# Chunk attention and a multiplicative FFN: tiles cut along the batches, more queries and keys loaded four tokens a partition, w1 and w2 awaited apart

## The chip, the cores and the metric

The kernel runs on one core of a Trainium2 chip. The metric is the device time of one execution in microseconds (us). The engines are TensorE (PE, matmuls, with PEld for its weight loads), VectorE (DVE), ScalarE (ACT), GpSimd (POOL, which here only issues loads) and SyncE (SP, which issues DMA transposes and stores). Sixteen DMA engines move the data.

## The reference, cut to what matters

```python
# q, k, v: (8, 8, 576, 64) float32: 8 batches, 8 heads, 576 tokens, 64 wide
q_c = q.reshape(B, H, 9, 64, D)                       # chunks of 64 tokens, 9 to a batch
scores = (1 / sqrt(D)) * matmul(q_c, k_c.transpose(0, 1, 2, 4, 3))
scores = scores - max(scores, axis=-1, keepdims=True)
attn = exp(scores); attn = attn / (sum(attn, -1) + 1e-9)
x = matmul(attn, v_c)            # each chunk attends to itself alone
x = x.transpose(0, 2, 1, 3).reshape(4608, 512)
h = ((x @ w1) * (x @ w2)) @ w3   # w1, w2: 512 x 1024, w3: 1024 x 1024
out = h @ w_out                  # w_out: 1024 x 512, out: 4608 x 512 float32
```

## The kernel before, in words

**Work.** A chunk is 64 tokens of one batch, and there are 72 of them. Two chunks make a *group* of 128 tokens (36 groups, g = 0 to 35), four groups make a *tile* of 512 tokens (9 tiles). In the kernel before, chunks are numbered straight through, so that a batch of nine chunks is four and a half groups, and a tile is eight chunks in a row wherever batches end: tile 0 is chunks 0 to 7 of batch 0, tile 1 is chunk 8 of batch 0 and chunks 0 to 6 of batch 1.

**A group.** Its queries and keys are brought in by POOL with a cast to bf16, turned so that the head dimension lies on the partitions, and copied: keys to `kT`, queries into `qd`, which holds two heads block-diagonally. Then PE makes the scores (`p_sc`, 8 matmuls), DVE takes the maximum and subtracts it, ACT the exponential, DVE the sum and the scaling to `an`; `an` is turned (`at`), PE multiplies by v (`p_av`, 8 matmuls with weights from `vd`, two heads block-diagonally), and ACT or DVE copies the result to `xt`, a ring of 16 groups.

**Two ways of loading q and k.** `load_qk` (L275) brings a group's q and k as one DMA each, one token a partition, so that DRAM is read in pieces of one head row (64 floats); a group that lies across two batches takes two halves each. `load_quad` (L289) brings eight chunks of four heads in four DMAs (two of k, two of q) with four tokens in a row on a partition (256 floats in a piece). A quad is turned by PE at L380: 16 matmuls on 64-column weights for k, and as many for q, serve two groups of the other cut (four chunks, four heads each). With `NQ = 1` tile 0 alone uses quads. Groups 4 to 11 are loaded by `load_qk` and turned by PE at L418 (8 matmuls a group); groups from 12 on are turned by DMA transposes (L422), and `an` from group 16 on too (L428).

**A tile.** `add_tile` (L577) makes for each of eight column blocks j the products a = x w1 and b = x w2 (L589: two *blocks* of four 128x512 matmuls), which ACT and DVE multiply into `abT`, and then four output products of eight matmuls (L620) with w3o = w3 w_out, copied by ACT or DVE and stored by SP (L630). w3o is made once at the start, from eight blocks w3 (L545 turns, L556 multiplies: 64 matmuls).

**What sets the order.** `Plan.run` lays the whole program out before it is built: each operation has engines, a cost and a key, and a list scheduler with modelled DMA queues picks the order in which each engine gets its instructions (and, where two engines can do an operation, which one does). On the chip every engine runs its list in order and waits by semaphores. POOL's loads follow the hand-written list `LOADS`, then a loop of q, k and v. Eight loads at most are on their way on POOL: a load waits for the landing of the eighth before it. `FLOWN` is the time at which the plan thinks that the DMA engines start. Until the first `p_av` matmul the plan puts filling matmuls on zeros (L683) into PE's longer gaps.

**What an operation waits for.** `w12_got[j]` holds one load for both w1 and w2: the last DMA of `load_w12`, which is w2's second half. A product waits for it and for `x_done` of the tile's four groups. A `p_av` waits for the v of its batch, which `load_v` brings in two DMAs of 64 partitions with all nine chunks. Stores wait until the q and k of group 35 were loaded. Tokens of groups 0 to 15 are kept for the store in the buffers of w3, w_out and `rawq` once these are free, later ones in 18 buffers `o_sb`.

Of the kernel before, what the change touches and what calls it, by code (L numbers as in the profile page):

```python
# [30 lines left out]
FLOWN, QUEUED, LAG = 3.5, 3.4, 1.2  # L31
# [143 lines left out]
def kernel(  # L175
# [32 lines left out]
    NG = N_TOK // (2 * C)  # L208
    scale = 1.0 / math.sqrt(D)
# [4 lines left out]
    BUFS = {"raw": 6, "rawq": 2, "kqT": 4, "kT": 3, "qd": 3, "vd": 3, "sd": 2, "e": 2, "an": 4, "at": 6, "w3t": 2, "abT": 2,  # L214
            "a_sb": 3, "o_sb": 18, "xt": XT, "ffn": 6, "p_sc": 1, "p_av": 1}
# [53 lines left out]

    def chunks(g):  # L270
        return [divmod(2 * g + cc, NCH) for cc in range(2)]
# [17 lines left out]
    def load_quad(n, y):  # L289
        box = quads[n, y] = {"ops": []}  # L290
        c0 = 8 * n
        cut = min(8, (c0 // NCH + 1) * NCH - c0)
        parts = [(c0, 0, cut)] + ([(c0, cut, 8)] if cut < 8 else [])
        for w, src in ((1, k), (0, q)):
            for t in range(2):
                for c, i0, i1 in parts:
                    def emit(eng, w=w, src=src, t=t, i0=i0, i1=i1):
                        if "t" not in box:
                            box["t"] = rawqs[len(turned_in) % len(rawqs)]
                            turned_in.append(box)  # L300
                        b, c = divmod(c0 + i0, NCH)
                        h = NM * t + 2 * y
                        nc.gpsimd.dma_start(box["t"][i0 * C // R:i1 * C // R, w, t],
                                            src[b, h:h + 2, c * C:(c + i1 - i0) * C, :].rearrange("h (p r) d -> p h (r d)", r=R))
                    box["ops"].append(load(0.084 * (i1 - i0), 0.5 + 0.02 * (i1 - i0), emit, takes=() if box["ops"] else ("rawq",)))

    def load_v(b, y0, y1):
        for t in range(2):
            def emit(eng, t=t):
                nc.gpsimd.dma_start(vds[b % len(vds)][halves[t], 2 * y0:2 * y1, :, t * D:(t + 1) * D].rearrange("p m c d -> p (m c) d"),  # L310
                                    v[b, NM * t + 2 * y0:NM * t + 2 * y1].rearrange("h (c p) d -> p (h c) d", p=C))
            o = load(1.07 * (y1 - y0), 0.5 + 0.335 * (y1 - y0), emit, takes=() if b in v_first else ("vd",),
                     after=(zero_v[b % len(vds)],))
            v_first.setdefault(b, o)
            for y in range(y0, y1):
                v_got.setdefault((b, y), []).append(o)

    def load_w12(j0, j1):
        for dst, w in ((w1_sb, moe_w1), (w2_sb, moe_w2)):
# [6 lines left out]
        for j in range(j0, j1):  # L326
            w12_got[j] = o
# [34 lines left out]
    def add_group(g, kt, ks, ka, kv):  # L362
# [3 lines left out]
        bc = [divmod(8 * n + 4 * hf + i, NCH) for i in range(4)] if quad else chunks(g)  # L366
# [34 lines left out]
        def quad_av(eng):  # L401
            t = box["av"] = ps("p_av", [P, 2, 4, C])
            for cc, (b, c) in enumerate(bc):
# [173 lines left out]
    def add_tile(g0, n, kab, ko_):  # L577
# [33 lines left out]
        for tk, x0, x1 in cols:  # L611
# [104 lines left out]
```

## Time and profile before

| | |
|---|---|
| runs | 249.84, 248.67, 249.61 us, median 249.61 |
| profiled execution | 249.81 us, its span 248.0 us (1.8 us lie around the span) |
| PE busy | 239.6 us of the span (97%), 1801 matmuls |
| DVE, ACT, POOL busy | 173.8, 146.3, 100.0 us |
| granted PE clock | 1.00 in every stretch |
| DMA | 38.58 MB, mean 156 GB/s |
| PE L589 (x w1, x w2) | 576 matmuls, 134.9 us busy |
| PE L620 (output) | 304 matmuls, 67.6 us busy |
| first L589 matmul, last L620 matmul's end | 36.9 us, 244.9 us |

Busy times of matmuls overlap, because they are pipelined: a 128x512 matmul is listed with 379 ns, while a row of them starts one every 0.216 us (the chain of waits has eight of them in 1.73 us). So where PE is at work, its work is counted here by the chain's pieces, and not by the busy column.

### The profile page before, as it was taken

Reading aid. Unit: us, or ns where it says so; the run is one execution under the profiler, and the core shown is the slowest. Engines: PE = TensorE matmul, PEld = TensorE weight load, DVE = VectorE, ACT = ScalarE, POOL = GpSimd, SP = SyncE. Lnnn points to the kernel's source line nnn. Section 1 sums busy time; section 2 is a strip of 40 time slices with the busy share of each in tenths; the row PEclk is TensorE's granted clock in tenths of the full one; section 3 lists DMA queues with packets and bytes.
Section 4 is the critical chain, followed back from the end, with each engine's and each line's share of the span. In section 5 each row is a group of like instructions: output and inputs, shape, how many; then the busy total and the mean of one; then the engine's idle time right before and its main releaser. Section 6 shows DMA issues by size and latency. Waiting matters only on the chain.

```text
span 248.0 us, 4765 instructions
## 1 busy us (share of the span) xinstructions
PE 239.6 (97%) x1801; PEld 123.6 (50%) x1801; DVE 173.8 (70%) x315; ACT 146.3 (59%) x250; POOL 100.0 (40%) x127
## 2 busy tenths in 40 slices
PE   7699999899999999999999999999999999999994
PEld 2455665456555554545545455454454544444443
DVE  6287879768988878987887778868888862332310
ACT  8566756656876775576566655565677544323222
POOL 8755889969773482274227435400000000000000
PEclk9999999999999999999999999999999999999999
DMA  7999999999999999999999999999469994121114
GB/s 196 194 203 173 177 182 180 166 155 148 132 135 144 158 154 157 137 156 138 156 136 161 130 156 156 146 148 161 86 140 307 342 344 144 45 84 42 45 42 169
DMA packets 154310, 38.58 MB, mean 156 GB/s; under 512 B 141232, under 2 KB 148272, under 8 KB 154288
## 3 DMA queue, kind: packets, MB, share of 16 engines
q0 software_dynamic: 112016, 18.88, 104.0%
q1 hardware_dynamic: 41984, 18.88, 40.6%
q10 hardware_dynamic: 288, 0.52, 0.8%
q8 instruction: 14, 0.23, 0.4%
q14 instruction: 8, 0.07, 0.1%
HBM read 38.80 MB, written 9.44 MB: 194 GB/s over the span
## 4 chain that ended last, share of the span: by engine, by line
PE 79%; DMA 10%; POOL 7%; issue 1%; DVE 1%; ACT 1%; POOLq 0%
PE ffn L589 45%; PE ffn L620 25%; DMA vd<-in_v_dram 7%; POOL w_sb L322 4%; PE p_av L490 3%; PE p_sc L447 3%; DMA rawq<-in_k_dram 2%; POOL raw L284 2%; POOL vd L310 1%; PE ffn L479 1%; PE p_av L683 1%; PE ffn L418 1%; ACT w3t L246 0%; PE ffn L380 0%; DVE qd L248 0%
## 5 line engine op out<-in xcount | busy, mean ns | idle before, releaser
L589 PE MATMUL ffn<-xt,w_sb 128*128 128x512 bf16 x576 | 134.9, 379 | 0.0
L589 PEld LDWEIGHTS <-w_sb 128*128 128x128 bf16 x576 | 53.7, 98 | 57.6
L598 DVE TENSOR_TENSOR abT<-a_sb,ffn 128x512 bf16<-128x512 f32 x72 | 48.8, 682 | 35.0 <-PE ffn L589 33.9
L620 PE MATMUL ffn<-w3o_sb,abT 128*128 128x512 bf16 (+2 forms) x304 | 67.6, 368 | 0.0
L246 ACT COPY a_sb<-ffn 128x512 f32<-128x512 f32 x72 | 42.0, 585 | 35.6 <-PE ffn L589 35.3
L284 POOL DMA_DIRECT2D raw<-in_q_dram x36 | 30.6, 854 | 43.5 <-DMA kqT<-raw 25.6
L620 PEld LDWEIGHTS <-abT 128*128 128x128 bf16 x304 | 28.3, 98 | 30.1
L284 POOL DMA_DIRECT2D raw<-in_k_dram x36 | 30.8, 860 | 9.0 <-DMA vd<-in_v_dram 6.8
L468 DVE TENSOR_REDUCE ss<-e 128x8 f32<-128x520 bf16 x36 | 24.8, 689 | 4.5 <-ACT e L464 4.4
L452 DVE TENSOR_REDUCE nm<-p_sc 128x8 f32<-128x512 f32 x36 | 24.3, 676 | 4.7 <-PE p_sc L447 4.0
L464 ACT ACTIVATE e<-sd 128x512 bf16<-128x512 f32 x36 | 22.8, 634 | 4.6 <-DVE sd L460 3.5
L474 DVE TENSOR_TENSOR an<-e,rs 128x512 bf16<-128x512 bf16 x36 | 24.7, 685 | 0.4
L246 ACT COPY o_sb<-ffn 128x512 f32<-128x512 f32 (+2 forms) x18 | 9.7, 539 | 22.3 <-PE ffn L620 22.2
L246 ACT COPY qd<-kqT 64x512 bf16<-64x512 bf16 x36 | 22.1, 614 | 0.2
L460 DVE TENSOR_TENSOR sd<-p_sc,nm 128x512 f32<-128x512 f32 x32 | 21.8, 682 | 0.4
L246 ACT CAST xt<-p_av 128x512 bf16<-128x512 f32 x27 | 15.9, 588 | 9.1 <-PE p_av L490 7.3
L310 POOL DMA_DIRECT2D vd<-in_v_dram x16 | 18.6, 1173 | 1.7 <-DVE ss L468 1.0
L556 PE MATMUL ffn<-wo_sb,w3t 128*128 128x512 bf16 x64 | 15.7, 380 | 0.2
L490 PEld LDWEIGHTS <-vd 128*128 128x128 bf16 x256 | 11.4, 98 | 6.3 <-issue 0.6
L447 PEld LDWEIGHTS <-qd 128*128 128x128 bf16 x256 | 11.2, 98 | 5.7 <-ACT qd L246 0.5
L490 PE MATMUL p_av<-at,vd 128*128 128x64 bf16 x256 | 12.8, 193 | 0.5 <-DMA vd<-in_v_dram 0.5
L248 DVE CAST xt<-p_av 128x512 bf16<-128x512 f32 x9 | 6.2, 689 | 5.9 <-PE p_av L490 5.9
(53 smaller groups left out, 164.4 us busy)
## 6 DMA issues: line engine op xcount, KB each, us to landing
out_dram<-o_sb SPq DMA_DIRECT2D x19, 256.0 KB, 2.4
vd<-in_v_dram POOLq DMA_DIRECT2D x16, 288.0 KB, 12.1
raw<-in_q_dram POOLq DMA_DIRECT2D x28, 128.0 KB, 9.0
raw<-in_k_dram POOLq DMA_DIRECT2D x28, 128.0 KB, 8.6
w_sb<-in_moe_w_dram POOLq DMA_DIRECT2D x8, 256.0 KB, 8.3
w_sb<-in_moe_w_dram POOLq DMA_DIRECT2D x16, 128.0 KB, 5.4
out_dram<-w_sb SPq DMA_DIRECT2D x8, 256.0 KB, 4.5
out_dram<-wo_sb SPq DMA_DIRECT2D x4, 256.0 KB, 2.8
```

Of the source, the lines that this page charges most:

```text
L246: nc.scalar.copy(o, i)
L284: nc.gpsimd.dma_start(box["t"][r, w], src[b, :, c * C:(c + n) * C, :].rearrange("h p d -> p h d"))
L310: nc.gpsimd.dma_start(vds[b % len(vds)][halves[t], 2 * y0:2 * y1, :, t * D:(t + 1) * D].rearrange("p m c d -> p (m c) d"), v[b, NM * t + 2 ...
L452: nc.vector.tensor_reduce(nm[:, :, 0], box["sc"], axis=AX.X, op=ALU.max)
L460: nc.vector.tensor_sub(sd[:], box["sc"], box["nm"].to_broadcast([P, 8, C]))
L464: nc.scalar.activation(e[:, :, :C], box["sd"][:], ACT.Exp, scale=scale)
L468: nc.vector.reduce_sum(ss[:], box["e"][:], axis=AX.X)
L474: nc.vector.tensor_mul(an[:], box["e"][:, :, :C], box["rs"].to_broadcast([P, 8, C]))
L490: nc.tensor.matmul(t[:, m, cc, :], vds[b % len(vds)][:, m, c, :], box["at"][:, 2 * cc + y, u * C:(u + 1) * C], start=True, stop=True)
L589: nc.tensor.matmul(t[:, :w], wt[:, ki, j * P:(j + 1) * P], x[:, ki, :], start=(ki == 0), stop=(ki == KO - 1))
L598: nc.vector.tensor_mul(box["abT"][:, j, :w], box["as", j][:, :w], box["b", j][:, :w])
L620: nc.tensor.matmul(t[:, :x1 - x0], box["abT"][:, ki, tk * P:(tk + 1) * P], w3o_sb[:, ki, x0:x1], start=(ki == 0), stop=(ki == FO - 1))
```

## The change

- `rows` and the new `chunks` cut tiles along the batches. Tiles 0 to 6 and tile 8 are the first eight chunks of one batch each (tile 8 is batch 7); tile 7 (`LEFT`) gathers the ninth chunk of all eight batches. Each group of tile 7 has chunks of two batches, so its q and k come in halves (16 DMAs, as the four groups across two batches took before), and its output rows are stored in two DMAs of 64 rows each.
- v is held by tile. The eight ordinary tiles load it as before, with all nine chunks of the batch; tile 7 loads its ninth chunks again, in eight small DMAs.
- `NQ = 3`: tiles 0, 1 and 2 (groups 0 to 11) use quads. `rawq` has four buffers in place of two, which also keep four more groups of output, and `o_sb` has 12 in place of 18.
- `w12_got` has an entry for w1 and one for w2, and each product waits for its own.
- `LOADS` has another order, and `FLOWN` is 2.7 in place of 3.5.

In the changed file the lines from 206 on stand some 2 to 12 lower: L380 becomes L391, L589 L600, L620 L631, L310 L325, L322 L333.

On PE the order that the plan makes has before the first product of tile 0: all of w3o as before, four L391 turns of sixteen matmuls more (quads 1,0 and 1,1, each k and q) in place of three L418 turns of eight, and the same four `p_av` of tile 0. The plan's fillers are 14 at the start, then 4 (7 before) between the first quad's k and q, then 2, 2 and 3 (2, 1 and 1 before). The first part of POOL's list, with DMAs in brackets, is: quad 0,0 (4); w3 three times; w_out (1); w3; quad 0,1 (4); w3; quad 1,0 (4); w3 twice; v of batch 0 (2); w3; w1 and w2 columns 0-1 (4); quad 1,1 (4); columns 2-3 (4); v of batch 1 (2); columns 6-7 (4); columns 4-5 (4); quad 2,0 (4); quad 2,1 (4); q and k of group 12 (2); v of batch 2 (2). Each set of w1 and w2 columns has w1's two DMAs first.

```diff
-LOADS = [('quad', 0, 0), ('w3', 5, 6), ('w3', 6, 7), ('ident',), ('wo', 4, 8), ('w3', 1, 2), ('quad', 0, 1), ('w3', 4,
-         5), ('w3', 0, 1), ('w3', 2, 3), ('v', 0, 0, 2), ('qk', 4), ('w3', 7, 8), ('w3', 3, 4), ('qk', 6), ('qk', 5),
-         ('w12', 0, 2), ('w12', 2, 4), ('w12', 6, 8), ('qk', 7), ('w12', 4, 6), ('v', 1, 0, 2), ('qk', 8), ('qk', 9),
-         ('qk', 10)]
+LOADS = [('quad', 0, 0), ('w3', 5, 6), ('w3', 7, 8), ('w3', 4, 5), ('ident',), ('wo', 4, 8), ('w3', 1, 2), ('quad', 0,
+         1), ('w3', 0, 1), ('quad', 1, 0), ('w3', 3, 4), ('w3', 6, 7), ('v', 0, 0, 2), ('w3', 2, 3), ('w12', 0, 2),
+         ('quad', 1, 1), ('w12', 2, 4), ('v', 1, 0, 2), ('w12', 6, 8), ('w12', 4, 6), ('quad', 2, 0), ('quad', 2, 1),
+         ('qk', 12)]
-NQ = 1
+NQ = 3
-FLOWN, QUEUED, LAG = 3.5, 3.4, 1.2
+FLOWN, QUEUED, LAG = 2.7, 3.4, 1.2
...
+    def rows(n):
+        return [(i, NCH - 1) for i in range(B)] if n == LEFT else [(n - (n > LEFT), c) for c in range(NCH - 1)]
+
     def chunks(g):
-        return [divmod(2 * g + cc, NCH) for cc in range(2)]
+        return rows(g // 4)[g % 4 * 2:g % 4 * 2 + 2]
...
         for w, src in ((1, k), (0, q)):
             for t in range(2):
-                for c, i0, i1 in parts:
...
+                def emit(eng, w=w, src=src, t=t):
+                    if "t" not in box:
+                        box["t"] = rawqs[len(turned_in) % len(rawqs)]
+                        turned_in.append(box)
+                    h = NM * t + 2 * y
+                    nc.gpsimd.dma_start(box["t"][:, w, t], src[n, h:h + 2, :R * P, :].rearrange("h (p r) d -> p h (r d)", r=R))
+                box["ops"].append(load(0.672, 0.66, emit, takes=() if box["ops"] else ("rawq",)))
...
+            if n == LEFT:
+                for m in range(2 * y0, 2 * y1):
+                    def emit(eng, t=t, m=m):
+                        nc.gpsimd.dma_start(vd[halves[t], m, :B, t * D:(t + 1) * D],
+                                            v[:, NM * t + m, (NCH - 1) * C:, :].rearrange("b p d -> p b d"))
+                    part(0.48, 0.62, (m // 2,), emit)
...
-        for j in range(j0, j1):
-            w12_got[j] = o
+            for j in range(j0, j1):
+                w12_got[name, j] = o
...
-            dep = [w12_got[j]] + [x_done[g0 + i] for i in range(n)] + ([first] if j else [])
-            a = plan.add("PE", 0.216 * n, kab(j), mm("a", w1_sb), after=dep, lag=0.2,
+            dep = [x_done[g0 + i] for i in range(n)] + ([first] if j else [])
+            a = plan.add("PE", 0.216 * n, kab(j), mm("a", w1_sb), after=dep + [w12_got["a", j]], lag=0.2,
...
             def o_out(eng, tk=tk, x0=x0, x1=x1):
-                r0 = (g0 + tk) * P
-                nc.sync.dma_start(out[r0:r0 + P, x0:x1], box["os", tk, x0][:, :x1 - x0])
+                os, bc = box["os", tk, x0][:, :x1 - x0], chunks(g0 + tk)
+                for i, (b, c) in enumerate(bc if bc[0][0] != bc[1][0] else bc[:1]):
+                    r0, n = b * S + c * C, P if bc[0][0] == bc[1][0] else C
+                    nc.sync.dma_start(out[r0:r0 + n, x0:x1], os[i * n:(i + 1) * n])
```

More of the change, by code (lines that the diff above doesn't have):

```diff
@@ L208 @@
     NG = N_TOK // (2 * C)
+    LEFT = 7
+    assert TT == (NCH - 1) * C == B * C
     scale = 1.0 / math.sqrt(D)
@@ L212 @@
     f32 = mybir.dt.float32
-    BUFS = {"raw": 6, "rawq": 2, "kqT": 4, "kT": 3, "qd": 3, "vd": 3, "sd": 2, "e": 2, "an": 4, "at": 6, "w3t": 2, "abT": 2,
-            "a_sb": 3, "o_sb": 18, "xt": XT, "ffn": 6, "p_sc": 1, "p_av": 1}
+    BUFS = {"raw": 6, "rawq": 4, "kqT": 4, "kT": 3, "qd": 3, "vd": 3, "sd": 2, "e": 2, "an": 4, "at": 6, "w3t": 2, "abT": 2,
+            "a_sb": 3, "o_sb": 12, "xt": XT, "ffn": 6, "p_sc": 1, "p_av": 1}
     consts = ctx.enter_context(tc.tile_pool(name="consts", bufs=1))
@@ L365, in add_group @@
         n, y, hf = g // 4, g % 4 // 2, g % 2
-        bc = [divmod(8 * n + 4 * hf + i, NCH) for i in range(4)] if quad else chunks(g)
+        cs = [4 * hf + i for i in range(4)] if quad else [g % 4 * 2, g % 4 * 2 + 1]
         qd = qds[g % len(qds)]
```

55 lines of the change are left out of this document (23 added, 32 removed).

## The prediction

> **What bounds the kernel now.** I read the page's busy shares and slices first, then PE's waits, the timelines of PE and POOL in the first 55 us, and the chain.
>
> ```profile
> PE 239.6 (97%) x1801; PEld 123.6 (50%) x1801; DVE 173.8 (70%) x315; ACT 146.3 (59%) x250; POOL 100.0 (40%) x127
> ...
> PEclk9999999999999999999999999999999999999999
> DMA  7999999999999999999999999999469994121114
> ```
>
> PE is the bound, at a full granted clock. The chain of waits names PE L589 and L620 without a break from 53 us on: the output product of tile 0 is at 55.5, the last L620 matmul ends at 244.9. Adding up PE's pieces at the chain's own durations (eight 128x512 matmuls 1.73, eight score or p_av matmuls 0.23, four turns of `an` 0.22, eight L418 turns 0.45, sixteen L380 turns 0.59, eight w3 turns 0.46) gives 190.0 us of work between 54.6 and the end, where 190.3 pass. No time can be won there except by taking PE work away, and the change takes none away. What can be won lies before 54.6:
>
> ```profile
> 7.28 0.41 PE L380 MATMUL ffn<-ident,rawq 128*64 128x128 bf16 x8 [1.58 <-DMA rawq<-in_k_dram]
> 7.92 0.41 PE L380 MATMUL ffn<-ident,rawq 128*64 128x128 bf16 x8 [0.22 <-DMA rawq<-in_k_dram]
> 8.26 1.68 PE L683 MATMUL p_av<-zeros 128*128 128x512 bf16 x7
> 9.88 0.64 PE L380 MATMUL ffn<-ident,rawq 128*64 128x128 bf16 x16
> ...
> 12.10 0.41 PE L398 MATMUL p_sc<-kT,qd 128*128 128x64 bf16 x8 [0.60 <-DVE qd L248]
> ...
> 44.69 0.62 PE L418 MATMUL ffn<-ident,raw 128*128 128x128 bf16 x8 [0.72 <-DMA raw<-in_k_dram]
> ...
> 52.63 0.28 PE L490 MATMUL p_av<-at,vd 128*128 128x64 bf16 x4 [0.51 <-DMA vd<-in_v_dram]
> ```
>
> The first quad's q landed at 9.30 (its last DMA is issued at 3.48 and takes 5.8), yet its turn began at 9.9, behind seven fillers of 0.22. By the same adding up, from the first turn at 7.28 to 54.63 PE had 40.1 us of work in 47.4: it lost 2.1 up to 9.95, 1.7 up to 17.1 (first copies, w_out), 1.6 up to the first product at 36.9, and 1.9 in tile 0's sixteen blocks, where the q and k of group 7 and the v of batch 1 came late. That v was late because POOL was late:
>
> ```profile
> 26.89 2.63 POOL raw L284 x3
> 29.52 1.86 POOL w_sb L322 x3
> ...
> 42.30 1.14 POOL vd L310
> 43.44 9.05 DMA vd<-in_v_dram
> ```
>
> From 26.9 to 43.4 the chain runs through POOL's issues, one after the other (0.88 for a q or k, 0.65 for w1 or w2), with the v at their end.
>
> **PE work, added.** Groups 4 to 11 lose eight L418 turns (8 x 0.45 = 3.6) and get four quads' turns of k and q (8 x 0.59 = 4.7): +1.1 us on the bound, hidden by nothing. Score, p_av, copy and softmax instructions stay in number and size (quad copies of `qd` took 0.42 on DVE at 10.56, plain ones 0.42 in the mean). The number of fillers stays 25. The Trainium skill (TensorE: Matmul & The Clock Gate, Weight-path perf modes) says that fast weight load is on "when the number of weights is 128", and these turns load 64; its slow rate, columns/1.2 ns, would make sixteen turns 0.85 us, by which the added turns would cost 3.2 in place of 1.1 and the forecast below would be 250.5. The trace disagrees on the size (0.59 for sixteen), though its loads of 64 columns do take longer than those of 128 (110 ns against 98), and 0.59 is used.
>
> **When the loads land.** The spacing of landings in the trace (issue plus time to landing, of single DMAs): quad 0.66, w3 block 1.25, half of w_out 2.54, v DMA 2.14, w1 or w2 0.67, q or k of a group 0.85. These sums give 51.4 for v of batch 1 in the kernel before, where 52.5 is measured, so they are good to about 1 us. In the new order: first quad 9.3 as now; w3 at 10.5, 11.8, 13.0; w_out 15.5; w3 16.8; quad 0,1 k and q 18.1, 19.5; w3 20.7; quad 1,0 22.1, 23.4; w3 24.7, 25.9; v of batch 0 30.2; w3 31.5; columns 0-1 w1 and w2 32.9, 34.2; quad 1,1 35.5, 36.9; columns 2-3 38.2, 39.6; v of batch 1 43.9; columns 6-7 45.2, 46.6; columns 4-5 47.9, 49.2; quad 2,0 50.6, 51.9; quad 2,1 53.2, 54.6; group 12 56.3; v of batch 2 60.6 (before: 60.2 and 64.3). POOL's chain is cut: between the v of batch 0 and that of batch 1 it issued 20 us of instructions, now 9.
>
> **PE's new order against these.** Four fillers in place of seven end at 9.25, so the q turn starts at 9.3: 0.6 won. The first scores follow at about 11.6 (12.1 before), after three serial copies of `qd`. The second half of the first w3o product waits for w_out as before; the first turn of `an` comes at 17.4. Then 19.2 us of work (48 product matmuls, 5 w3 turns, 6 quad turns, 5 of `an`, 4 scores, 4 p_av) and 0.9 of fillers and the wait around them bring the first product of tile 0 to 37.6; on the way each load is there 0.3 to 0.9 before its use, only quad 1,1's q is 0.1 late. The sixteen blocks with two scores, three turns of `an`, three p_av and the turns of quad 2,0 are 16.8 us: 54.3. On the way block 9 needs w1 of columns 6-7 at 45.3 (landed 45.2), block 11 its w2 at 47.5 (46.6), block 12 w1 of columns 4-5 at 48.4 (47.9), block 13 its w2 at 49.5 (49.2), quad 2,0 is turned at 51.2 (50.6). Awaiting w1 apart is what lets blocks 9 and 12 start; with w2 awaited too block 9 would start at 46.6, 1.3 us later, most of what this stretch wins.
>
> At 54.3 the new order has done one `an` turn, two p_av and quad 2,0 more than the old one had at 54.63, and has no four L418 left but quad 2,1: 190.3 - 0.22 - 0.46 - 1.8 + 1.18 = 189.0 are left. PE would end at 243.3, not 244.9: **-1.6 us**, the added 1.1 paid. This counts almost no loss from 17 to 54, where the kernel before lost 1.6 and 1.9. From below: none of it comes back. From above: all 3.5 comes back, and the result is +1.9. The nearest row is 27 to 42 of the same trace, with loads there in time, where PE lost about 0.3; I take 0.2.
>
> **Later.** Scores of groups 12 to 17 need DMA transposes; their q, k and v land about 4 us earlier, PE comes 1.6 earlier: covered. One place is tight: `an` of group 16 was ready 5.7 after its scores and took 8.4 to turn on SP's queue; the plan now puts its p_av 13.4 after the scores (19.8 before). That is a wait of 0 to 0.7; I take 0.2. PE is in order, so the wait stops everything behind it once.
>
> Tile 7: eight small v DMAs more (halves land 0.42 to 0.48 apart: 3.4 us of DMA, about 5.6 of POOL's issues against 2.3), four stores more on SP (0.6 each). At nothing: POOL ends at 160 us, the v of batch 7 had landed 20 us ahead of its p_av, and SP issued a store every 5.2 us from 205 on. Without that cover they would cost up to 3.4 and 2.2. The four `o_sb` groups of tile 8 need stores of tile 5, 60 us before. The tail (last matmul 244.9, span 248.0) has the same instructions.
>
> **Sum.** The profiled execution took 249.81: -1.6 + 0.2 + 0.2 = -1.2 gives 248.6. That execution is 0.2 above the median of the runs, so the forecast for the median is **248.4**.
>
> **Rivals.** *The waits only move.* The new order was made for loads that land just in time, and DVE stays at some 85% (by my count 18 us of its work from 37.6 to 58.9). If the loads are 1 to 2 us later, or DVE delays an `an` or a freed buffer, PE loses 1 to 2 of the 1.6 and the time is 249.0 to 250.2. For it: slacks under 1 us; columns 4-5 land 2 us later than before. Against: POOL's chain is gone.
>
> *Eight in flight bind, and the kernel is slower.* POOL's load waits for the landing of the eighth before it; the trace shows this at 12.02 and 14.57. From columns 0-1 to quad 2,1 stand 28 small DMAs. With a time to landing of 5.0 (w1 and w2 at 34 us) plus 0.3 to wake POOL, eight in flight give one per 0.66, just what I used. The first quad took 5.8: 0.76 apiece, 2.5 late at the end, and after the slack 1.7 to 1.9 of wait, 249.9. From a time to landing of 6.1 on (0.80 apiece, 3.7 late, 2.9 of wait) it is slower by over 0.5%; at 6.5, 252.2. For it: quads behind others took 8.7. Against: that was in a full queue, which loses nothing.
>
> **How the numbers follow.** This kernel's runs spread over 0.5%, which is about what can be told from no change. Forecast 0.55 (247.6 to 248.9; 0.44 of it under 248.36), waits only move 0.25 (all within 0.5%), eight in flight 0.20 (250.8 to 252). Faster 0.44, same 0.36, slower 0.20. The range from 247.6, with no loss and the fillers' wait too, to 250.9 leaves out most of the last case.
>
> **What would show it.** Right: the q turn at 9.3, first L600 near 37.6, v of batch 1 landed near 44, tile 0's output product near 56 with three tiles' turns ahead, last L631 matmul near 243.7, and L391 groups of 16 in 0.59. Wrong: waits of PE on rawq or w1/w2 loads over 1 us between 20 and 56 (the rivals), POOL idle behind landings with DMA engines not full (eight in flight), or PE waits on `at` after 100 us.

## The result: one per cent slower, and the profile after

| | before | after |
|---|---|---|
| median of six runs each | 249.5 us (248.67 to 249.84) | 251.92 us (251.26 to 252.61) |
| ratio, 95% interval | | 1.0104 [1.0075, 1.0133] |
| profiled execution | 249.81 us | 252.45 us |
| its span, and what lies around it | 248.0 + 1.8 | 250.2 + 2.25 |
| last output matmul ends | 244.9 | 246.88 |

The forecast was 248.4, the range 247.6 to 250.9. The kernel became 2.4 us slower where 1.2 were to be won, and the time lies outside the range, in the direction that had a chance of 0.20, though not by the mechanism that had been given for it: that the number falls into that rival's 250.8 to 252 is chance. The ratios here and below leave out runs that lie more than 1.5% above the fastest of the same kernel, which are three of e5's twelve (253.56, 253.68 and 255.09 us).

The busy shares and slices on the page of the changed kernel:

```profile
PE 241.7 (97%) x1865; PEld 123.3 (49%) x1865; DVE 176.3 (70%) x321; ACT 143.5 (57%) x244; POOL 102.8 (41%) x135
...
PEclk9999999999999999999999999999999999999999
DMA  7999999999999999999999999995757997122114
```

PE is the bound as before, at the full granted clock (1.00); its busy time is 2.1 us longer. Where the time went is read from the timeline of PE (start, duration, and in brackets the idle time before it). These are the changed kernel's lines; L391 turns a quad, L556 turns a w3 block, L567 multiplies w3o, L600 is the product with w1 or w2:

```profile
8.13 1.04 PE L695 MATMUL p_av<-zeros 128*128 128x512 bf16 x4
9.10 0.64 PE L391 MATMUL ffn<-ident,rawq 128*64 128x128 bf16 x16
...
11.92 0.41 PE L409 MATMUL p_sc<-kT,qd 128*128 128x64 bf16 x8 [0.87 <-ACT qd L248]
...
17.34 0.39 PE L490 MATMUL ffn<-ident,an 128*128 128x128 bf16 x4
18.60 0.62 PE L556 MATMUL ffn<-ident,w_sb 128*128 128x128 bf16 x8 [0.87 <-DMA w_sb<-in_moe_w_dram]
...
24.69 1.04 PE L567 MATMUL ffn<-wo_sb,w3t 128*128 128x512 bf16 x4
25.65 0.64 PE L391 MATMUL ffn<-ident,rawq 128*64 128x128 bf16 x16
26.22 1.04 PE L567 MATMUL ffn<-wo_sb,w3t 128*128 128x512 bf16 x4
27.10 0.40 PE L409 MATMUL p_sc<-kT,qd 128*128 128x64 bf16 x8
...
28.19 1.06 PE L556 MATMUL ffn<-ident,w_sb 128*128 128x128 bf16 x16
29.09 0.81 PE L695 MATMUL p_av<-zeros 128*128 128x512 bf16 x3
30.40 0.39 PE L409 MATMUL p_sc<-kT,qd 128*128 128x64 bf16 x8 [0.51 <-DVE sd L468]
...
38.88 0.64 PE L391 MATMUL ffn<-ident,rawq 128*64 128x128 bf16 x16
39.45 2.76 PE L600 MATMUL ffn<-xt,w_sb 128*128 128x512 bf16 x12
...
46.42 2.19 PE L600 MATMUL ffn<-xt,w_sb 128*128 128x512 bf16 x8
48.45 0.40 PE L416 MATMUL p_av<-at,vd 128*128 128x64 bf16 x8
...
51.73 2.19 PE L600 MATMUL ffn<-xt,w_sb 128*128 128x512 bf16 x8
```

The q turn is at 9.10 and the first turn of `an` at 17.34, as forecast (9.3 and 17.4). Then four things are to be seen. At 18.60 PE had waited 0.87 for a w3 block by the idle column; counted from the end of the turn of `an` at 17.56 (17.34 and 0.22) it is 1.04. The product of four at 24.69 takes until 25.65, 0.96, where a turn of a quad stands behind it; the same four at 26.22 take 0.88 where scores follow. Between 29.09 and 30.40 PE did nothing for the result: three fillers, then a wait, for the scores of group 4. And the eight matmuls at 46.42 took 2.03 until the next instruction, where eight in a row take 1.73. So the first product of tile 0 came at 39.4 (forecast 37.6; before 36.9), and the sixteenth ended at 57.0 (forecast 54.3).

The chain that ended last, in order of time, no longer goes through POOL's issues to the v of batch 1, as it did before; that v landed at 45.37 in place of 52.5. It names what took their place:

```profile
7.37 11.18 DMA w_sb<-in_moe_w_dram
...
25.72 0.59 PE ffn L391 x16
26.33 0.59 ACT qd L248
26.94 0.42 DVE qd L250
27.37 0.77 DVE qd L250 x2
28.17 0.69 DVE nm L463
28.86 0.61 DVE ss L479
29.70 0.57 DVE sd L468
30.40 0.39 PE p_sc L409 x8
...
46.59 0.45 PE ffn L600 x2
47.06 0.70 DVE xt L250
47.80 0.81 PE ffn L600 x3
```

First a w3 load; then, behind the turn of the q of quad 1,0, four copies to `qd`, one on ACT and three on DVE, and behind them on DVE the maximum, a sum and the subtraction of earlier groups, because there is one buffer for scores (`p_sc`) and the subtraction is what frees it. And twice in tile 0's products (the second time at 52.79) a copy of *tile 1's* x (groups 4 and 6), on which those products do not depend by their arithmetic.

### The profile page after: what moved, and what is told of

Read it like the earlier page. It is cut to its first block, busy times and chain, and to the rows that moved or that the text cites. A ratio compares the mean times of both kernels' runs of the same rounds, so it can differ in the third digit from the quotient of the medians.

```text
span 250.2 us, 4918 instructions
## 1 busy us (share of the span) xinstructions
PE 241.7 (97%) x1865; PEld 123.3 (49%) x1865; DVE 176.3 (70%) x321; ACT 143.5 (57%) x244; POOL 102.8 (41%) x135
## 4 chain that ended last, share of the span: by engine, by line
PE 88%; DMA 4%; POOL 2%; DVE 2%; ACT 1%; issue 1%; POOLq 0%
PE ffn L600 49%; PE ffn L631 25%; DMA w_sb<-in_moe_w_dram 4%; PE ffn L567 4%; PE p_sc L458 2%; PE p_av L501 2%; PE ffn L391 2%; PE ffn L490 1%; PE p_av L416 1%; POOL rawq L303 1%; PE p_sc L409 1%; DVE qd L250 1%; ACT qd L248 1%; POOL w_sb L342 1%; PE ffn L556 1%
## 5 line engine op out<-in xcount | busy, mean ns | idle before, releaser
L600 PE MATMUL ffn<-xt,w_sb 128*128 128x512 bf16 x576 | 135.6, 379 | 0.3
L600 PEld LDWEIGHTS <-w_sb 128*128 128x128 bf16 x576 | 53.3, 98 | 57.6 <-issue 0.7
L631 PE MATMUL ffn<-w3o_sb,abT 128*128 128x512 bf16 (+2 forms) x304 | 67.6, 368 | 0.0
L248 ACT COPY a_sb<-ffn 128x512 f32<-128x512 f32 x72 | 42.0, 584 | 38.7 <-PE ffn L600 38.5
L631 PEld LDWEIGHTS <-abT 128*128 128x128 bf16 x304 | 28.7, 98 | 31.8
L289 POOL DMA_DIRECT2D raw<-in_q_dram x28 | 23.7, 851 | 33.6 <-DMA kqT<-raw 30.5
L289 POOL DMA_DIRECT2D raw<-in_k_dram x28 | 23.9, 857 | 6.7 <-DMA vd<-in_v_dram 6.4
L248 ACT COPY o_sb<-ffn 128x512 f32<-128x512 f32 (+2 forms) x15 | 7.9, 528 | 21.6 <-PE ffn L631 21.6
L248 ACT COPY qd<-kqT 64x512 bf16<-64x512 bf16 x32 | 19.7, 616 | 0.3
L325 POOL DMA_DIRECT2D vd<-in_v_dram x16 | 18.7, 1182 | 2.6 <-PE ffn L600 1.7
L471 DVE TENSOR_TENSOR sd<-p_sc,nm 128x512 f32<-128x512 f32 x24 | 16.4, 685 | 0.3
L250 DVE CAST xt<-p_av 128x512 bf16<-128x512 f32 x16 | 11.0, 687 | 8.0 <-PE p_av L501 6.5
L567 PE MATMUL ffn<-wo_sb,w3t 128*128 128x512 bf16 x64 | 16.3, 380 | 0.0
L248 ACT CAST xt<-p_av 128x512 bf16<-128x512 f32 x20 | 11.7, 587 | 5.5 <-PE ffn L600 2.9
L303 POOL DMA_DIRECT2D rawq<-in_k_dram x12 | 8.6, 722 | 7.0 <-DMA vd<-in_v_dram 2.4
L501 PEld LDWEIGHTS <-vd 128*128 128x128 bf16 x192 | 8.7, 98 | 5.0 <-issue 0.2
L333 POOL DMA_DIRECT2D w_sb<-in_moe_w_dram x16 | 9.9, 643 | 2.4 <-DMA vd<-in_v_dram 2.3
```

What stands on the lines that cost most here:

```text
L248: nc.scalar.copy(o, i)
L289: nc.gpsimd.dma_start(box["t"][r, w], src[b, :, c * C:(c + n) * C, :].rearrange("h p d -> p h d"))
L325: nc.gpsimd.dma_start(vd[halves[t], 2 * y0:2 * y1, :, t * D:(t + 1) * D].rearrange("p m c d -> p (m c) d"), v[b, NM * t + 2 * y0:NM * t + ...
L471: nc.vector.tensor_sub(sd[:], box["sc"], box["nm"].to_broadcast([P, 8, C]))
L567: nc.tensor.matmul(box["wp"][:], box["t"][:, ki, :], wo_sb[:, ki, :], start=(ki == wo_cut[0][0]), stop=(ki == wo_cut[-1][1] - 1))
L600: nc.tensor.matmul(t[:, :w], wt[:, ki, j * P:(j + 1) * P], x[:, ki, :], start=(ki == 0), stop=(ki == KO - 1))
```

## The experiments

Four reasons stood against each other, for the front of the kernel (up to the end of tile 0's products) above all: *the loads land late* (by my sums v and w1/w2 should have landed 1.4 to 1.9 us earlier than they did); *DVE's chain* of copies and softmax ahead of group 4's scores; *false waits*, in which products of tile 0 wait for the copy of tile 1's x; and *the parts*, that one of the three parts of the change is itself a loss. Later came the price of a quad's turn. Each ratio is to runs of the kernel before that were timed beside it (medians 249.23 us for e1 to e4, 249.22 for e5 to e8, 248.84 for e9 to e12, 249.70 for e13 to e15), so that the ratios, and not the medians, are to be compared. Where an edit changes what an operation waits for or which loads there are (e4 to e7, e12), the plan also lays out the whole order anew.

**False waits: x in four buffers (e1).** `xt` is one buffer for four tiles, and a quad's copy writes a strided piece of it, which stretches over columns of another tile.

```diff
-    xt = wpool.tile([P, NM, XT * P], bf, tag="xt")
+    xts = [wpool.tile([P, NM, TT], bf, tag=f"xt{i}", name=f"xt{i}") for i in range(XT // 4)]
```

> The changed kernel with xt as four buffers of one tile each in place of one buffer of four tiles; nothing else moves, the order on every engine stays. Theory X (false waits): in the changed kernel two products of tile 0 stand still in the middle of a block, at 47 and 53 us, until DVE has copied x of groups 4 and 6, which they do not read; a quad's copy is a strided region, and the wait is made for the whole stretch of the buffer between its ends. By X the two stops of 0.46 us go and some small ones later: -0.9 us or a little more, about 250.9. Rival C (DVE and ACT set the pace): PE comes 0.9 earlier to waits for copies and softmax that stay where they are; under -0.3 us.

Measured: 251.45 us (250.65 to 251.77), 1.0085 [1.0054, 1.0115] of before. On PE's timeline the two stopped groups of products are whole again:

```profile
45.48 1.89 PE L600 MATMUL ffn<-xt,w_sb 128*128 128x512 bf16 x7
...
50.48 1.89 PE L600 MATMUL ffn<-xt,w_sb 128*128 128x512 bf16 x8
```

From the first product to the end of the sixteenth it is 17.0 us, not 17.6. So the false waits are real, and cost 0.6 us in the trace; in the time 0.5 (1.0104 to 1.0085), which the intervals do not tell apart from nothing. They are about a sixth of the 3.5 us that were missing, and not the 0.9 that was expected of them. That it is the strided copy which does it is borne out by the kernel before: there plain copies of the next tile's x go into the same one buffer beside a tile's products, and no group of products stops in the middle.

**The same split in the kernel before (e8).**

> The kernel before with xt in four buffers, no order changed. Theory X: its x copies of other groups stand in the same way behind products, but all of tile 0's quads were copied before its products, and from 55 us on PE lost 0.3 us in all; so -0.3 to 0: 249.2 to 249.5. If the split itself helped in general (rival: it is no cure of the change's loss but of both kernels), -0.9 as in the changed kernel.

Measured: 249.1 us, 0.9986 [0.9971, 1.0002]. There the split gives nothing that can be told from no change: what fits is that the stretch overlaps only where quads of tile 1 are copied while tile 0's products run.

**Lighter loads (e2, e3).** Half of the columns of w_out's second half are not loaded but set to zero at the start; e2 is the changed kernel with this, e3 has the split as well.

```diff
-        nc.gpsimd.dma_start(wo_sb[:, k0:k1, :], moe_w_out.rearrange(...)[:, k0:k1, :])
+        nc.gpsimd.dma_start(wo_sb[:, k0:k1, :D_MODEL // 2], moe_w_out.rearrange(...)[:, k0:k1, :D_MODEL // 2])
...
+        nc.vector.memset(wo_sb[:, STAGED:, D_MODEL // 2:], 0.0)
```

> The changed kernel, but the second half of w_out is loaded with 256 of its 512 columns (the others are set to zero once at the start), so that all loads behind it land about 1.2 us earlier; no order changes. Theory L (the loads are late): in the changed kernel w3 block 1 lands at 18.55 in place of the 16.8 that I had added up, and everything behind is 1.1 to 2.1 us late, while the order left 0.3 to 0.9 us. By L the first product comes at 38.3 in place of 39.4 and the time falls by 0.9 to 1.3 us, to about 250.8. Rival C (serial copies and softmax on DVE and ACT before the score of group 4 at 30.4 set the pace): at most -0.3 us.

> Both of the edits before together: xt in four buffers, and half of the columns of w_out's second half left unloaded. If X and L each take their own stretch of the front, the gains add: about -2.0 us, 249.9. If both only bring PE earlier to one common wait (C), the sum is no more than the larger of the two.

Measured: e2 252.67 us, 1.0141 [1.0109, 1.0173]; e3 252.16 us, 1.0107 [1.0068, 1.0146]. Neither gained what was expected (250.8 and 249.9), and neither is a clean test: a quarter of `wo_sb` is cleared at the start, and the first quad's q landed 0.35 us later than in the changed kernel in e2's profile and 1.5 later in e3's. The 0.35 is no more than executions differ without this edit (8.55 in e9, 9.30 in before). What can be read is inside the profiles. In e2 the loads behind w_out landed 0.8 to 2.7 us earlier than in the changed kernel's profile up to the v of batch 1 (44.44; a w3 block at 15.83 in place of 18.55), and still the first product came at 38.6, where e1, with its loads not lightened, had it at 38.5. Counted from the first scores (12.25 in e2, 13.42 in e3, 11.83 in e1) it is 26.3 us in e2 and e3, and 26.7 in e1. So lighter loads were worth about 0.4 in the front, not the 0.9 to 1.3 that the loads alone should have given.

**Cleaner: DVE's order (e9), less of w3 (e10), both (e11).** All three have x in four buffers. In e9 the list of DVE is changed behind the plan, so that the two copies for group 5 no longer stand ahead of group 3's maximum, and the three fillers ahead of group 4's scores are left out:

```diff
+        late = [o for o in order if tag(o) == ("qd", 5)]
+        for o in late:
+            order.remove(o)
+        at = [tag(o) for o in order].index(("sd", 3)) + 1
+        order[at:at] = late
...
-                    fills = int((o.start - last - 0.2) / 0.25)
+                    fills = int((o.start - last - 0.2) / 0.25) if last < 20 else 0
```

In e10 w3's fourth block is loaded for 128 of its 1024 columns, and its turn reads the second block instead:

```diff
+            n = P if k0 == 3 else D_FF
+            nc.gpsimd.dma_start(w3_sb[:, k0:k1, :n], moe_w3.rearrange("(ko p) n -> p ko n", p=P)[:, k0:k1, :n])
...
+                nc.tensor.transpose(t[:, ki, :], w3_sb[:, 1 if ko == 3 else ko, ki * P:(ki + 1) * P], ident[:])
```

> The changed kernel with x in four buffers (251.45 us, first product of tile 0 at 38.5, sixteenth block's end 55.2) and one change of order on DVE: the two copies of qd for group 5 come behind the subtraction of group 3 instead of ahead of its maximum, and the three filling matmuls ahead of group 4's scores are left out. Theory 'DVE holds the front' (the scores of group 4, at 29.46, waited 1.3 us, fillers and wait together, for p_sc, which DVE emptied late because the copies stood ahead): scores of group 4 near 28.6, the first product near 37.7, the time near 250.6. Rival 'loads hold the front' (the q of quad 1,1 landed at 37.59 and its turn began at 37.93): group 4's scores are earlier by the same 0.9, but the wait comes back at the q turn of quad 1,1, the first product stays within 0.2 of 38.5 and the time within 0.3 of 251.4.

> The changed kernel with x in four buffers, of w3's fourth block only the first 128 columns loaded (that block's turn reads the second block instead, so the output is not the reference's): 1.1 us of DMA less, from 26 us on, and nothing else moved on PE, ACT or DVE. Loads hold the front: everything from the v of batch 0 on lands 1.1 earlier, the first product comes at 37.5 to 37.7 and the time is about 250.5. DVE holds the front: the first product stays at 38.4 to 38.5 and the time within 0.3 of 251.4.

> Both edits together (part of w3 not loaded, so the output is not the reference's). If DVE and the loads each hold the front at about the same time, each edit alone gives nearly nothing and both give the first product at 37.5, the sixteenth block's end at 54.2 and 250.3 us; if one of them alone holds it, this is that edit's time to 0.3 us.

Measured, with the first scores of each profile, since the first quad does not land at the same time in every execution (where a trace lacks the record of the first product's first matmul, as in e1 and e10, its place is 0.22 ahead of the first one listed):

| | time, ratio | first scores | group 4's scores | first product | from first scores to it |
|---|---|---|---|---|---|
| e1 | 251.45, 1.0085 [1.0054, 1.0115] | 11.83 | 29.46 | 38.5 | 26.7 |
| e9 | 251.09, 1.0092 [1.0068, 1.0115] | 11.38 | 28.34 | 38.0 | 26.6 |
| e10 | 250.73, 1.0075 [1.0053, 1.0096] | 12.03 | 29.38 | 38.4 | 26.4 |
| e11 | 250.69, 1.0071 [1.0052, 1.0090] | 11.93 | 28.74 | 38.2 | 26.3 |
| changed kernel | 251.92, 1.0104 [1.0075, 1.0133] | 11.92 | 30.40 | 39.4 | 27.5 |

In e9 group 4's scores are 0.7 earlier, counted from the first scores, and hardly any of it is left at the first product. PE's timeline of e9 shows where it went:

```profile
28.34 0.41 PE L409 MATMUL p_sc<-kT,qd 128*128 128x64 bf16 x8 [0.42 <-DVE sd L468]
28.63 1.04 PE L569 MATMUL ffn<-wo_sb,w3t 128*128 128x512 bf16 x4
29.83 0.40 PE L490 MATMUL ffn<-ident,an 128*128 128x128 bf16 x4 [0.16 <-DVE an L485]
...
37.43 0.64 PE L391 MATMUL ffn<-ident,rawq 128*64 128x128 bf16 x16
38.00 2.76 PE L602 MATMUL ffn<-xt,w_sb 128*128 128x512 bf16 x11
```

The next turn of `an` is late in its place (1.20 from 28.63 to 29.83, where the four matmuls are 0.87), and the last quad turn stands right behind its load, which landed at 37.38. So neither theory holds alone: each edit shortens the front by 0.1 to 0.3 us, both by 0.4 where 1.0 was expected, and the times of the three cannot be told apart. With both, the front needs 26.3 us where the forecast had 26.0 (11.6 to 37.6); from the first turn of `an` to the first product it is 20.9, the forecast 20.2. DVE's chain and the loads are two gates set close behind each other; they are not where most of the 3.5 us went. The one large wait for a load, 0.87 at 18.60, is the changed kernel's profile alone: that w3 block landed at 18.55 there, and at 16.3 to 16.8 in e1, e9, e10 and e11.

**The price of a quad's turn (e13, e14).** 32 more turns, one ahead of each product with w1 in tiles 3 to 6, written into the PSUM buffer that the product then overwrites; in e13 each is sixteen matmuls with 64 columns of weights, as at L391, in e14 eight with 128 columns, as at L418 of before.

```diff
...
+                    if name == "a" and 12 <= g0 < 28:
+                        tr = t.bitcast(bf)
+                        for i in range(8):
+                            for u in range(2):      # e13
+                                nc.tensor.transpose(tr[halves[u], i * P:(i + 1) * P], ident[:, u * C:(u + 1) * C], ident[:])
+                            nc.tensor.transpose(tr[:, i * P:(i + 1) * P], ident[:], ident[:])      # e14, in place of the two lines above
```

> The changed kernel with x in four buffers (251.4 us) and 32 more turns, one ahead of each product with w1 in tiles 3 to 6, where PE is the bound: sixteen matmuls with 64 columns of weights each, as a quad's turn has, written into the PSUM buffer that the product then overwrites. If a quad's turn costs 0.57 to 0.59, as the prediction took it, the time rises by 18.2 to 18.9 us to about 270; if it costs 0.67, because whatever stands ahead of it takes 0.10 longer, it rises by 21.4 to 272.8.

> The same with 32 turns of eight matmuls with 128 columns of weights each, as a turn of load_qk's groups has: 0.45 a turn by the rows, so 14.4 us more, about 265.8, by either theory. The difference to the run with 64 columns, divided by 32, is what one quad's turn costs above one plain turn: 0.12 to 0.14 by the prediction's rows, 0.22 with the gap.

Measured: e13 272.09 us, 1.0914 [1.0869, 1.0959]; e14 265.35 us, 1.0615 [1.0567, 1.0663]. From the first product to PE's last matmul it is 206.6 us in e1, 228.3 in e13, 220.9 in e14: 0.68 for a turn with 64 columns, 0.44 for one with 128, a difference of 0.23 (by the ratios 0.65, 0.41 and 0.23). The rows on PE's timeline, e13 and then e14:

```profile
112.10 0.64 PE L603 MATMUL ffn<-ident 128*64 128x128 bf16 x16
112.67 1.90 PE L605 MATMUL ffn<-xt,w_sb 128*128 128x512 bf16 x8
...
114.64 1.89 PE L636 MATMUL ffn<-w3o_sb,abT 128*128 128x512 bf16 x8
116.46 0.64 PE L603 MATMUL ffn<-ident 128*64 128x128 bf16 x16
```

```profile
114.03 1.89 PE L635 MATMUL ffn<-w3o_sb,abT 128*128 128x512 bf16 x8
115.76 0.61 PE L602 MATMUL ffn<-ident 128*128 128x128 bf16 x8
116.20 1.89 PE L604 MATMUL ffn<-xt,w_sb 128*128 128x512 bf16 x8
```

Eight output matmuls are listed with 1.89 in both, but the turn with 64 columns begins 1.82 after they began, the turn with 128 columns 1.73 after. So the turn lengthens what stands ahead of it by 0.09 to 0.10, which no idle column shows; with the 0.57 from its own start to the next start that is 0.67. (Behind nine of the 32 turns e13's timeline lists an idle 0.16; there the record of the next product's first matmul is missing, seven listed for eight or three for four, so this is no wait.) The prediction's 0.59 is the turn's own piece in the chain and leaves the lengthening out. The two runs differ in the number of instructions as well as in the width of the weights, so they give the price of a turn and not which of the two sets it.

**Group 16's p_av later (e15).** To take away the reason for the one wait that the prediction called tight, e9's program with the p_av of group 16 and its copy behind three more blocks.

```diff
+        av, x = ([tag(o) for o in order].index((n, 16)) for n in ("av", "x"))
+        later = [i for i in range(av + 1, len(order)) if order[i].engine == "PE"][3]
+        pair = [order[av], order[x]]
+        order[later + 1:later + 1] = pair
+        order = [o for i, o in enumerate(order) if o not in pair or i > later]
```

> The changed kernel with x in four buffers and the copies of group 5 later (251.1 us), and the p_av of group 16 with its copy moved behind three more blocks on PE (2.6 us). In the profile of the run without this move PE waited 0.77 us at 107.4 for the DMA transpose of group 16; in other profiles of this order 0 to 0.17. If that wait is in most runs, the time falls by 0.4 to 0.8, to about 250.5, and the scatter shrinks; if it is rare, the time stays at 251.1.

Measured: 251.39 us, 1.0076 [1.0046, 1.0105], against 1.0092 [1.0068, 1.0115] for e9: not told apart. The wait for the transpose is gone from the profile, and another stands 4 us behind. From PE's timelines, e9:

```profile
107.44 0.39 PE L501 MATMUL p_av<-at,vd 128*128 128x64 bf16 x8 [0.77 <-DMA at<-an]
```

and e15:

```profile
112.98 0.39 PE L458 MATMUL p_sc<-kqT,qd 128*128 128x64 bf16 x8 [0.95 <-ACT e L475]
```

The loss came back at the scores of a later group: the same work, from the output product at 101.95 in e9 or 100.80 in e15 to the second one after it (at 114.17 and 113.21), takes 12.2 us in e9 and 12.4 in e15, and 11.3 in the changed kernel's profile (103.13 to 114.42), where neither wait is there. So by execution this place costs 0 to about 1 us.

**The parts.** e4 is the changed kernel with w1 and w2 awaited together:

```diff
-            a = plan.add(..., after=dep + [w12_got["a", j]], ...)
+            a = plan.add(..., after=dep + [w12_got["b", j]], ...)
```

> The changed kernel with one wait for both w1 and w2 again: each product of x w1 waits for w2's last load too; the loads keep their order, PE's order in tile 0 changes a little with the plan. The prediction's working said that awaiting w1 apart saves 1.3 us at block 9. In the profile w2 of columns 6-7 landed at 48.1 and block 9 stood at 47.8 for a false wait, so theory X says that the part was worth 0.3 to 0.8 us: 252.2 to 252.7. By the prediction's step: 253.2.

Measured: 253.19 us, 1.0147 [1.0118, 1.0176]. Awaiting them apart is worth 1.1 us by the ratios (1.3 by the medians) inside the change, as the prediction's step had it (1.3); the two intervals overlap a little.

e7 is the kernel before with nothing but this part:

> Only the third part: the kernel before with w1 and w2 awaited apart. In its profile the products of tile 0 lost 1.9 us, 0.9 of it to a load of q and k and 0.7 to the v of batch 1, neither of which moves; w1 and w2 landed before use. So 249.5, within 0.3 us. Rival: the plan moves products forward and takes up the gaps: -0.5 us.

Measured: 250.76 us, 1.0066 [1.0042, 1.0090]. Alone the same part is a loss of 1.6 us, where nothing or a small gain was expected. The plan now draws four of tile 0's products ahead of w3o's last four (the first comes at 35.9, 0.9 earlier than in before), and PE then waits for scores, which in before waited for nothing (the waits of PE in e7):

```profile
PE p_sc L447 <- DVE sd L460: 1.0, 1, 1.0
```

In e7's profile PE's last matmul ends 0.8 later than before's. The same wait, 1.01 at 39.91, stands in the profile of e12, below, which has this part with before's loads too.

e5 has the new cut of the tiles alone (the changed code with quads for tile 0 only, before's load order, buffers and `FLOWN`, w1 and w2 awaited together), e12 the same with w1 and w2 awaited apart, e6 the kernel before with `NQ = 3`, four `rawq`, twelve `o_sb`, and the new load order and `FLOWN`, but the old cut.

```diff
-NQ = 3
+NQ = 1
-FLOWN, QUEUED, LAG = 2.7, 3.4, 1.2
+FLOWN, QUEUED, LAG = 3.5, 3.4, 1.2
```

> Only the new cut of the tiles: the changed kernel with quads for tile 0 alone, the loads in the order of the kernel before, w1 and w2 awaited together, o_sb and rawq as before. Tile 7's eight small v loads and its stores in halves are in it. The prediction put the cut at nothing: 249.5, within 0.3 us. Rival: the 1 MB of extra v and the halves cost DMA time that PE waits for: 250 to 251.

> Quads for tile 0 alone and the loads in the order of before, but tiles cut along the batches and w1 and w2 awaited apart. The cut alone (with both awaited together) gave 251.3 with a wide scatter; awaiting apart gained 1.3 inside the changed kernel and cost 1.3 alone in the kernel before. If the cut costs 1.8 and awaiting apart is bad with the old loads: 252.6. If awaiting apart gains with the new cut: 250.0. What the changed kernel's 251.9 stands above or below it is what the quads of tiles 1 and 2 with the new load order are worth; by the prediction they gain 1 us or more, by the rows of the turns (0.67 each with the gap ahead of it) they cost 1.8 of PE work against 3.6 taken away by nothing.

> Only the quads: the kernel before with its old cut, but quads for tiles 0 to 2, the new order of loads, FLOWN 2.7, four rawq and twelve o_sb. w1 and w2 are awaited together. Quads that lie across two batches are loaded in more and smaller DMAs. Theory: the quads with their loads carry the whole loss (1.1 us of PE turns and 1 to 2 us of late loads): 251.5 to 253, as the changed kernel or worse. If the cut carries it: 249.5 to 250.

| | new cut | quads for three tiles, new loads | w1, w2 apart | time, ratio |
|---|---|---|---|---|
| e5 | yes | | | 251.33, 1.0074 [1.0049, 1.0099] |
| e7 | | | yes | 250.76, 1.0066 [1.0042, 1.0090] |
| e6 | | yes | | 256.83, 1.0304 [1.0278, 1.0330] |
| e12 | yes | | yes | 253.59, 1.0190 [1.0153, 1.0226] |
| e4 | yes | yes | | 253.19, 1.0147 [1.0118, 1.0176] |
| changed kernel | yes | yes | yes | 251.92, 1.0104 [1.0075, 1.0133] |

Every part alone is slower than before, and so is every pair that was run; e5, e6 and e7 all came out slower than expected. The cut costs 1.8 us by itself, where the prediction had it at nothing. e5's twelve runs (all of them in the median, nine in the ratio) scatter from 249.75, the level of before, to 255.09, and the profiled one is the last of these: it waited 2.7 us for an `an` and 1.6 for a group's k, and whether the others did is not known. So where the cut's cost arises stays open. In e12 PE waits for the transposes of group 16:

```profile
109.33 0.39 PE L501 MATMUL p_av<-at,vd 128*128 128x64 bf16 x8 [1.18 <-DMA at<-an]
```

and its tiles 3 to 8 take 113.6 us from first product to first product, where before's and the changed kernel's both take 112.2. On the new cut, with w1 and w2 apart, the quads and loads gain 2.1 us (1.0190 to 1.0104); with w1 and w2 together they cost 1.8 (1.0074 to 1.0147), and on the old cut 7.6. So what a part is worth depends on the others, but the three together are no better than the cut or the wait apart by itself (1.0104 beside 1.0074 and 1.0066, the intervals overlap), and 2.4 us behind the program that they replace.

## Why the prediction was wrong, step by step

The prediction's sum for the profiled execution was 248.6 (PE's end at 243.7, with the two allowances of 0.2), and it took 252.45. The 3.8 us between, by the prediction's own steps:

| step | forecast | profile after | missed |
|---|---|---|---|
| first product of tile 0 | 37.6 | 39.45 | 1.85 |
| from it to the sixteenth's end | 16.7 | 17.6 | 0.9 |
| from there to PE's end, allowances included | 189.4 | 189.8 | 0.4 |
| from PE's end to the span's | 3.1 | 3.3 | 0.2 |
| around the span | 1.8 | 2.25 | 0.4 |

**The step that failed** is "This counts almost no loss from 17 to 54 ... I take 0.2". The sum was made of PE's pieces laid end to end, with the loads as the only thing that could come between, and the 0.2 was taken from a stretch of 15 us of the old program that had no quad turns and no copies of a second quad in it. The bound "From above: all 3.5 comes back, and the result is +1.9" was none: the profiled execution took 2.6 more than before's, because what came was for the most part not the old losses. From the first turn of `an` to the first product PE took 22.1 where 20.2 were forecast, and the 1.9 us are 1.0 for the w3 block at 18.60, 0.4 at group 4's scores (1.3 for 0.9) and 0.5 for six quad turns (0.67 for 0.59). The 0.9 in the sixteen blocks are 0.6 of false waits, 0.2 of two turns' lengthening and 0.1 without a name; the 0.4 behind them, 0.2 of two more turns and a third stop, 0.19 at 83.05 behind a copy of x, that e1's trace does not have. That is one execution, 0.5 above the median, and its 1.0 for the w3 block is not in four other profiles of the same order. The items one by one:

- **The term of the turns was mis-sized.** "Four quads' turns of k and q (8 x 0.59 = 4.7)" against "8 x 0.45": +1.1 was counted. A turn costs 0.68 in place (e13) and a plain one 0.44 (e14): +1.9. For the six turns ahead of the first product, the two in the sixteen blocks and the two of quad 2,1 that is 0.9 us that the sums left out. The lengthening was in the trace of before, too (there L556 multiplies w3o, L380 turns a quad and L418 a plain group): four matmuls on w_out at 18.77 ran until the quad's turn at 19.74, 0.97, and the four at 32.27 until the plain turn at 33.14, 0.87. I had looked at the turn and not at its neighbour.

```profile
18.77 1.04 PE L556 MATMUL ffn<-wo_sb,w3t 128*128 128x512 bf16 x4
19.74 0.64 PE L380 MATMUL ffn<-ident,rawq 128*64 128x128 bf16 x16
...
32.27 1.04 PE L556 MATMUL ffn<-wo_sb,w3t 128*128 128x512 bf16 x4
33.14 0.61 PE L418 MATMUL ffn<-ident,raw 128*128 128x128 bf16 x8
```

  The Trainium skill (TensorE: Matmul & The Clock Gate, Weight-path perf modes) ties the fast weight load to 128 weights. The prediction weighed this rule and set its 250.5 aside on the size of one row; the rule had the direction right, and the estimate that the prediction worked out from the Trainium skill's columns/1.2 ns (same page, LDWEIGHTS: 0.85 for sixteen loads) is above the 0.68 that the runs show. No run here shows that the fast load is the reason, since the turns differ in the number of instructions too.
- **False waits**, 0.6 us in the trace (46.42 and 51.73), shown by e1. The prediction did not have them in any case: tile 1's x is now copied by quads while tile 0 is being multiplied from the same buffer.
- **Group 4's scores** came 1.3 us after the last useful instruction, where "0.9 of fillers and the wait around them" were counted, and the loads stood close behind; e9 to e11 show that the two together are worth 0.4 in the front.
- **The landing sums** were 1.1 late by 20 us and 1.3 to 1.9 from 32 us on (v of batch 0 at 32.06 for 30.2, w1 of columns 0-1 at 34.28 for 32.9, v of batch 1 at 45.37 for 43.9). "Good to about 1 us" was too much trust, with slacks of 0.3 to 0.9 in the plan. The sums hold nothing for two DMA transfers of the kind `instruction` (16 KB, queue q8), at 16.48 and 29.26 in the changed kernel's trace: ahead of the first the w_out load was on time, behind it the loads are 1.1 late, and behind the second 1.3 or more. Which load is late first differs by execution. Here it was the w3 block, at 18.55 for 16.8, which cost the wait at 18.60; in e1, e9, e10 and e11 it was the load behind it, and PE did not wait for that one. So this largest single wait is bad luck of the profiled execution. That the transfers are what delays the loads fits these traces, but no run was made without them.
- **"At nothing" for the cut** was wrong as a claim on that part: alone it costs 1.8 us (e5), and where stays open. Inside the whole change tile 7 and its stores cost nothing that shows: tile 8 takes 27.8 us from its first product to PE's end, as it did before.
- **At group 16** the wait was put at "0 to 0.7; I take 0.2". It was 0 in the profiles of the changed kernel and of e1, 0.17 in e11, 0.77 in e9 and, with fewer quads, 1.18 in e12: the size was about right, and where it was taken away another came (e15).
- **0.3 us outside the span.** In nearly every run of the changed kernel and its relatives with three tiles of quads on the new cut about 2.1 us or more lie around the span, in before, e5, e6, e7, e8 and e12 1.7 to 1.9. No run here tells why.

**What was right:** the q turn (9.10 for 9.3) and the first turn of `an`; POOL's chain was cut and the v of batch 1 landed 7 us earlier than before; awaiting w1 apart is worth 1.1 to 1.3 us inside the change ("1.3 us later, most of what this stretch wins"; e4); the sixteen blocks took 17.0 without the false waits, 16.7 and 0.2 for two turns' gaps; tiles 3 to 8 ran at the old pace. Of the rivals, "The waits only move" had part of the mechanism (DVE and late loads) and its price too low: 1 to 2 us lost, where 3.8 were. "Eight in flight bind" gave the right side, but by a mechanism that the trace doesn't show. POOL did stand idle behind landings (2.40 ahead of 30.48, 1.42 ahead of 44.19), but the DMA engines were busy meanwhile (every slice reads 9 there), and the small loads from 36 us on landed mostly 0.65 to 0.75 apart, as counted.

With the false waits and DVE's order mended and part of a load left out (e11), the kernel stands at 1.0071 of before. The quad turns' price and the time outside the span are still in it; no run takes them away. No version run here can be told to be faster than the kernel before.

## What to carry to other kernels

A short operation's price is what the whole row grows by when it is put in: measure from the start of the instruction ahead of it to the start of the one behind it, in both neighbourhoods, because its cost can show in a neighbour's duration and in no idle column. When a forecast replaces an order that has measured losses by one that is only added up, some of the old losses must be carried over unless each has a named cause that is gone; here 3.5 us of them were counted as 0.2. And what one part of a change is worth can turn its sign with the other parts (w1 and w2 apart: 1.6 us lost in e7, 1.1 won inside the change), so a change of order is judged as a whole, against the program that was tuned with its own order.

## What the runs showed of the hardware that was not expected

- Sixteen transposes with 64 columns of weights cost 0.68 us in a PE-bound stretch where eight with 128 columns cost 0.44 for the same data (e13, e14; by the ratios 0.65 and 0.41); 0.57 of it stands from the turn's own start to the next, 0.10 in the row ahead of it.
- One load can land 1.8 us later in one execution than in another with its neighbours in place: the w3 block behind w_out landed at 18.55 in the changed kernel's profile and at 16.79 in e1's, while w_out ahead of it landed at 15.58 and 15.56, and the last DMA of the quad behind it at 20.57 and 20.22. In both traces a 16 KB `instruction` transfer of 0.94 us begins at 16.4 to 16.5, and one load that was due within 1 us of that transfer's end lands 1.1 to 1.7 late by its spacing: the w3 block in the one, the next load, a quad's k, in the other. Before's, e2's, e9's, e10's and e11's traces have such a late load too (by 0.5 to 1.4), e3's, with the transfer at 18.02, has none. That the transfer is the cause was not tried.
